# Keys of the last two token blocks as one product in seven half-size parts (Strassen), with both blocks' gates ahead of it

## The chip, the core and the metric

The kernel runs on one core of a Trainium2 chip. Times are device microseconds (us) of a whole execution; the number that counts is the median of several. In the profile PE is the matrix engine, PEld its weight loads, DVE the vector engine, ACT the scalar engine, POOL GpSimd, and SP the engine whose queue issues the DMAs.

## What is computed

Eight batches of a packed attention make `x` (4608 tokens of 512 channels), and a channel mix follows, whose products are the bulk of the work:

```python
x_prev = np.concatenate([zeros, x[:, :-1, :]], axis=1)
xk = mu_k * x + (1.0 - mu_k) * x_prev
xr = mu_r * x + (1.0 - mu_r) * x_prev
k = np.maximum(xk @ w_k, 0.0)              # 512 -> 1024: the keys
v = k * k @ w_v                            # 1024 -> 512: the values
r = 1.0 / (1.0 + np.exp(-(xr @ w_r)))      # 512 -> 512: the gates
return r * v
```

All in fp32. A factor that goes into a product is held as two fp32r parts, high and low, and a product is the sum of three matmuls: high by high, high by low, low by high.

## The kernel before

Tokens go in nine blocks of 512 (`TB`), numbered 0 to 8; channels in chunks of 128 (`P`). For a block, `gates(i)` makes 4 tiles of 4 chunks (48 matmuls with the three parts), `keys(i)` 8 tiles of 4 chunks (96), `values(i)` 4 tiles over 8 chunks (96): 240 matmuls of 128x512. `channel_mix` (L1267) runs gates, keys and values of block after block, and spawns the mixes of the next block (`mix`, `split`, L1091 and L1133) after the keys. A key tile `ph` is one bank of PSUM (a slot `m` of four); `squared` (L1169) then takes it by two ACT operations (L1173, L1176) and two on DVE (L1184, L1186) into `sq`, which `values` reads. `done` (L1247) multiplies a value tile by its gate on DVE (L1251) and issues the output DMA.

The attention of the batches is worked in between on the same engines and ends some 170 us before the kernel does. Its larger PSUM tiles, the two slots `pa`, are of two banks each: `banks(slot)` is `[P, 2, 512]`.

Nothing is scheduled at run time. `Flow` is a planner: each stage is a generator that yields an engine with an estimated duration, and the planner's estimates decide in which order the instructions are written, engine by engine. Each engine then runs its own instructions in that order and waits on semaphores which are put in from the tiles that an instruction reads and writes, in the order in which the instructions were written. A wait stands for all that follows on its engine.

Of the kernel before, what the change touches and what calls it, by code (L numbers as in the profile page):

```python
# [173 lines left out]
def attn_pack_channel_mix(ctx: ExitStack, tc: tile.TileContext, q, k, v, p, mu_k, mu_r, w_k, w_v, w_r, out):  # L174
    nc = tc.nc
    B, H, S, D = q.shape
    NP = p.shape[2]
    DM, DF = w_k.shape
    P = 128
# [5 lines left out]
    NC = DM // P  # L185
    NF = DF // P
    TB = 512
# [24 lines left out]
    def pe(us, after=None):  # L212
        return "tensor", us, after, None
# [877 lines left out]
    def mix(i, j, res, tag):  # L1091

        yield from flow.wait("mu")
        rank = flow.now.rank
        for c in range(NC):
            yield from flow.wait(*(
                e for b, *_ in pieces(i)
                for e in ([("xt", b, c, 0), ("xt", b, c, 1)] if b else [("kept", j // 2, c // 2)])
            ))
            slot = yield from flow.take("xk" if tag == "xk" else "sq")  # L1100

            space = "tmp"
# [49 lines left out]
    def keys(i):  # L1152
        for f in range(NF):
            slot = yield from flow.take("m")
            ph = ps.tile([P, 512], F32, name="ph", tag=f"m{slot}")[:, :TB]
            fs = slice(f * P, (f + 1) * P)
            for c in range(NC):
                yield from flow.wait(*made("xk", i, c), ("wk", c, f * P // WP * WP))
                yield pe(0.685)
                flow.now.t -= flow.LAG  # L1160
                _, xh, xl = xks[i, c]
                nc.tensor.matmul(ph, wk_h[:, c, fs], xh, start=(c == 0), stop=False)  # L1162
                nc.tensor.matmul(ph, wk_h[:, c, fs], xl, start=False, stop=False)  # L1163
# [3 lines left out]
            flow.spawn(squared(i, f, slot, ph), 0, flow.t + flow.LAG)  # L1167

    def squared(i, f, slot, ph):  # L1169
        sr = yield from flow.take("tmp")  # L1170
        r = tile_([P, WP], F32, "tmp", sr, "r")[:, :TB]
        yield act(TB)
        nc.scalar.activation(r, ph, AF.Relu)  # L1173
        flow.give("m", slot)
        yield act(TB)
        nc.scalar.activation(r, r, AF.Square)  # L1176
        sh = yield from flow.take("sq")
        hl = tile_([P, 2, TB], F32R, "sq", sh)
        if i < 1:
            yield act(TB, after=0.0)  # L1180
            nc.scalar.copy(hl[:, 0, :], r)  # L1181
        else:
            yield vec2(TB)
            nc.vector.tensor_copy(hl[:, 0, :], r)  # L1184
        yield vec(TB)
        nc.vector.tensor_tensor(hl[:, 1, :], r, hl[:, 0, :].bitcast(F32), op=ALU.subtract)  # L1186
        flow.give("tmp", sr)
        sqs[i, f] = sh, hl
        flow.set(("sq", i, f))
# [26 lines left out]
                flow.spawn(gated(i, x, slot, pr), 0, flow.t + flow.LAG)  # L1216

    def gated(i, t, slot, pr):
        sg = yield from flow.take("sig")
        sig = tile_([P, DM], F32, "sig", sg)  # L1220
        yield act(DM, table="sigmoid")
        nc.scalar.activation(sig, pr, AF.Sigmoid)  # L1222
        flow.give("m", slot)
        sigs[i, t] = sg, sig
        flow.set(("sig", i, t))

    def values(i):
        slots, pv = {}, {}
        for f in range(NF):
            yield from flow.wait(("sq", i, f), *(("wv", f, o) for o in range(0, DM, WP)))  # L1230
            sf, hl = sqs.pop((i, f))
            for t in range(NT):
# [12 lines left out]
            flow.give("sq", sf)  # L1245

    def done(i, t, slot, pv):  # L1247
        yield from flow.wait(("sig", i, t))
        sg, sig = sigs.pop((i, t))
        yield vec(DM)  # L1250
        nc.vector.tensor_tensor(sig, pv, sig, op=ALU.mult)  # L1251
        flow.give("m", slot)
        t0 = i * TB + t * P
        if t0 <= TB:

            runs_ = out[:S].rearrange("(r j) c -> j r c", j=RUN)
            for x, half in enumerate(HALVES):
# [7 lines left out]
        flow.give("sig", sg)  # L1265

    def channel_mix():  # L1267
        for i in range(NB):
# [4 lines left out]
            if i + 1 < NB:  # L1273
                mixes(i + 1)
            yield from values(i)

    def mixes(i):
        flow.spawn(mix(i, 2, xrs, "xr"), 1)
        flow.spawn(mix(i, 0, xks, "xk"), 1.1)

    def fronts():
        for b in range(B):
# [55 lines left out]
    flow.spawn(fronts(), 10)  # L1338
    weights()
    flow.spawn(shares(), 10.0)  # L1340
    flow.spawn(channel_mix(), 50)

    spare = ps.tile([P, 512], F32, name="spare", tag="m3")
# [31 lines left out]
```

## Time and profile before

| | us |
|---|---|
| runs, median of 3 (lowest to highest) | 590.94 (590.58 to 590.96) |
| span of the profiled execution, first to last instruction | 587.7 |
| median less that span | 3.2 |
| PE busy | 578.4 (98%) |
| DVE busy | 370.9 (63%) |
| ACT busy | 314.3 (53%) |

The time of the profiled execution itself is not among the runs; its span is, and the 3.2 us that the median has over it lie ahead of the first and behind the last instruction. PE's busy time counts a matmul from its start to its modelled end, and these overlap: the spacing of the starts is what an added or removed matmul costs. Idle time of the other engines costs nothing while PE has work.

### The profile page before, as it was taken

The numbers are of one execution on the slowest core, as the hardware profiler recorded it, in microseconds if no ns is written. First come the engines' busy times: TensorE is split into PE (matmuls) and PEld (weight loads), VectorE is DVE, ScalarE is ACT, GpSimd is POOL, SyncE is SP. The second block draws the span as 40 slices with busy tenths as digits, with TensorE's granted clock in tenths as the row PEclk, the third lists the DMA queues.
The fourth block names the chain that finished last, engine by engine and source line by source line (L and its number), as shares of the span: only waits on it lengthen the run. The fifth ranks groups of instructions, "written<-read, shape, count | busy, mean of one in ns | idle before, by whom it ended". The sixth has DMA issues, their size and how long they took to land.

```text
span 587.7 us, 10541 instructions
## 1 busy us (share of the span) xinstructions
PE 578.4 (98%) x4115; PEld 455.6 (78%) x4115; DVE 370.9 (63%) x702; ACT 314.3 (53%) x569; POOL 7.8 (1%) x33
## 2 busy tenths in 40 slices
PE   8999999999999999999999999999999999999997
PEld 7877777687788778777877777777788888888885
DVE  1999799956892888098828879559514713640321
ACT  5679974755744583368327654637535613721410
POOL 3000000000000000000000000000000000000000
PEclk9999999999999999999999999999999999999999
DMA  8987340863376365417621764820100010001001
GB/s 303 337 239 238 109 63 15 191 139 56 87 146 153 73 118 99 128 17 155 133 97 30 152 137 107 171 69 0 73 0 1 0 73 0 1 0 73 0 2 71
DMA packets 160593, 56.66 MB, mean 96 GB/s; under 512 B 136856, under 2 KB 150304, under 8 KB 160544
## 3 DMA queue, kind: packets, MB, share of 16 engines
q1 hardware_dynamic: 160224, 55.86, 37.8%
q8 instruction: 32, 0.52, 0.4%
q0 software_dynamic: 320, 0.14, 0.1%
q14 instruction: 17, 0.14, 0.1%
HBM read 43.00 MB, written 12.98 MB: 95 GB/s over the span
## 4 chain that ended last, share of the span: by engine, by line
PE 78%; DVE 13%; ACT 3%; DMA 3%; issue 2%; SPq 0%; DVEq 0%; ACTq 0%
PE ph L1162 10%; PE ph L1163 10%; PE ph L1164 10%; PE pvo L1240 9%; PE pvo L1242 9%; PE pvo L1241 9%; PE pr L1210 5%; PE pr L1212 5%; PE pr L1211 5%; PE pa L706 2%; DVE x L1117 2%; DVE m L303 2%; PE pa L898 1%; PE pa L672 1%; PE pa L841 1%
## 5 line engine op out<-in xcount | busy, mean ns | idle before, releaser
L1162 PE MATMUL ph<-xk,wk_h 128*128 128x512 f32 x288 | 115.6, 401 | 0.0
L1240 PE MATMUL pvo<-wv,sq 128*128 128x512 f32 x288 | 113.8, 395 | 0.0
L1163 PE MATMUL ph<-xk,wk_h 128*128 128x512 f32 x288 | 112.4, 390 | 0.0
L1164 PE MATMUL ph<-xk,wk_l 128*128 128x512 f32 x288 | 112.2, 390 | 0.0
L1241 PE MATMUL pvo<-wv,sq 128*128 128x512 f32 x288 | 112.2, 389 | 0.0
L1242 PE MATMUL pvo<-wv,sq 128*128 128x512 f32 x288 | 112.1, 389 | 0.0
L1184 DVE CAST sq<-r 128x512 fp32r<-128x512 f32 x64 | 27.0, 421 | 97.2 <-ACT r L1176 94.9
L1173 ACT ACTIVATE r<-ph 128x512 f32<-128x512 f32 x72 | 43.2, 600 | 77.8 <-PE ph L1164 75.7
L1162 PEld LDWEIGHTS ph<-xk,wk_h 128*128 128x128 f32 x288 | 54.0, 188 | 16.7 <-issue 5.9
L1240 PEld LDWEIGHTS pvo<-wv,sq 128*128 128x128 f32 x288 | 54.1, 188 | 16.0 <-issue 4.9
L1164 PEld LDWEIGHTS ph<-xk,wk_l 128*128 128x128 f32 x288 | 54.1, 188 | 11.4
L1242 PEld LDWEIGHTS pvo<-wv,sq 128*128 128x128 f32 x288 | 54.1, 188 | 11.3
L1241 PEld LDWEIGHTS pvo<-wv,sq 128*128 128x128 f32 x288 | 54.1, 188 | 10.7
L1163 PEld LDWEIGHTS ph<-xk,wk_h 128*128 128x128 f32 x288 | 54.2, 188 | 10.2 <-DVE xk L1056 0.2
L1210 PE MATMUL pr<-wr_h,xr 128*128 128x512 f32 x144 | 57.8, 402 | 0.7 <-ACT xr L1137 0.6
L1212 PE MATMUL pr<-wr_h,xr 128*128 128x512 f32 x144 | 56.3, 391 | 0.8 <-DVE xr L1139 0.8
L1211 PE MATMUL pr<-wr_l,xr 128*128 128x512 f32 x144 | 56.2, 390 | 0.0
L1117 DVE SCALAR_TENSOR_TENSOR x<-xt,mus,x 128x448 f32<-128x448 f32 (+6 forms) x112 | 52.4, 510 | 5.4 <-ACT x L1111 5.3
L1111 ACT ACTIVATE x<-xt,mus 128x448 f32<-128x448 f32 (+7 forms) x112 | 53.7, 527 | 2.4 <-DVE sq L1186 1.2
L1186 DVE TENSOR_TENSOR sq<-r,sq 128x512 fp32r<-128x512 f32 x72 | 49.1, 681 | 4.6 <-ACT sq L1181 3.3
L1222 ACT ACTIVATE sig<-pr 128x512 f32<-128x512 f32 x36 | 20.7, 598 | 54.2 <-PE pr L1212 42.1
L1176 ACT ACTIVATE r<-r 128x512 f32<-128x512 f32 x72 | 45.6, 633 | 1.7
(151 smaller groups left out, 679.5 us busy)
## 6 DMA issues: line engine op xcount, KB each, us to landing
out<-sig SPq DMA_DIRECT2D x31, 256.0 KB, 2.9
vt<-in_v SPq DMA_DIRECT2D x14, 512.0 KB, 4.9
raw<-in_k SPq DMA_DIRECT2D x96, 72.0 KB, 2.7
raw<-in_q SPq DMA_DIRECT2D x96, 72.0 KB, 2.8
st<-in_moe_w_k SPq DMA_DIRECT2D x8, 512.0 KB, 9.3
st<-in_moe_w_v SPq DMA_DIRECT2D x8, 512.0 KB, 5.7
far<-at SPq DMA_DIRECT2D x12, 288.0 KB, 2.6
aTd<-far SPq DMA_DIRECT2D x12, 256.0 KB, 2.9
```

The source lines that it names most:

```text
L1111: nc.scalar.mul(x32[:, o:o + n], xts[b, c][:, 1 + s:1 + s + n], mus[:, j, c:c + 1])
L1117: nc.vector.scalar_tensor_tensor(x32[:, o:o + n], xts[b, c][:, s:s + n], mus[:, j + 1, c:c + 1], x32[:, o:o + n], op0=ALU.mult, op1=ALU.add,)
L1162: nc.tensor.matmul(ph, wk_h[:, c, fs], xh, start=(c == 0), stop=False)
L1163: nc.tensor.matmul(ph, wk_h[:, c, fs], xl, start=False, stop=False)
L1164: nc.tensor.matmul(ph, wk_l[:, c, fs], xh, start=False, stop=(c == NC - 1))
L1186: nc.vector.tensor_tensor(hl[:, 1, :], r, hl[:, 0, :].bitcast(F32), op=ALU.subtract)
L1210: nc.tensor.matmul(pr, xh[:, ts_], wr_h[:, c, :], start=(c == 0), stop=False)
L1211: nc.tensor.matmul(pr, xh[:, ts_], wr_l[:, c, :], start=False, stop=False)
L1212: nc.tensor.matmul(pr, xl[:, ts_], wr_h[:, c, :], start=False, stop=(c == NC - 1))
L1240: nc.tensor.matmul(pv[t], sh, wvs[f][:, 0, :], start=(f == 0), stop=False)
L1241: nc.tensor.matmul(pv[t], sh, wvs[f][:, 1, :], start=False, stop=False)
L1242: nc.tensor.matmul(pv[t], sl, wvs[f][:, 0, :], start=False, stop=(f == NF - 1))
```

## The change

Take the two last blocks, 7 and 8, as one factor of 1024 tokens by 512 channels, in quarters: A11 and A12 are block 7's first and last 256 channels, and A21 and A22 block 8's. `w_k` is quartered alike (W11, W12, W21, W22, each 256 by 512). Instead of eight products of quarters there are seven, by Winograd's form of Strassen's scheme. S1 to S4 are sums of the A's, T1 to T4 sums of the W's; "pass" is one such product, 4 tiles of 2 chunks of 3 matmuls: 24 matmuls.

- `sums_of_w` makes T1 to T4 on DVE and ACT after the last batch's attention, in buffers that this has left free (T1 in the place of W12, which no pass reads).
- `quarters` replaces the mixes of both blocks: the gates' factors of both, then A in fp32, then the seven forms (A11, A12, S2, S3, S1, A22, S4) split in high and low on DVE. A form takes two `xt` slots, there are four: from the third on, a form can be written only when the pass two before it is done on PE.
- `channel_mix` runs, after block 6's values: gates of 7, gates of 8, the seven passes, values of 7, values of 8.
- `keys_of_pair` runs the passes. Those of Z go to four one-bank tiles (`ph`), those of X to the two two-bank tiles (`pa`), `X = [twin[j // 2][:, j % 2, :] for j in range(HF)]`. Some pass adds into a bank of an earlier one. What ACT keeps from Z (`kept`) DVE adds to X (`made_of`, three times four adds), and relu, square and split follow as before.
- The gates of block 8 stay in the `vt` buffers. No DMA is added or removed.

The core of the diff:

```diff
+        for i in PAIR:
+            yield from gates(i)
+        yield from keys_of_pair()
+        for i in PAIR:
+            yield from values(i)
...
+        yield from formed("A11", a)
+        yield from formed("A12", b)
+        forms["S2"] = yield from form_tiles()
+        for u in range(HC):
+            yield vec(TB)
+            nc.vector.tensor_tensor(c[:, u, :], a[:, u, :], c[:, u, :], op=ALU.subtract)
+            st_ = yield from flow.take("tmp")
+            s2 = tile_([P, TB], F32, "tmp", st_, "s2")
+            yield vec(TB)
+            nc.vector.tensor_tensor(s2, d[:, u, :], c[:, u, :], op=ALU.subtract)
+            yield from parted_form("S2", s2, u)
+            yield vec(TB)
+            nc.vector.tensor_tensor(a[:, u, :], a[:, u, :], s2, op=ALU.add)
+            yield vec(TB)
+            nc.vector.tensor_tensor(b[:, u, :], b[:, u, :], s2, op=ALU.subtract)
+            flow.give("tmp", st_)
+        for name, x, slot in (("S3", c, sc), ("S1", a, sa), ("A22", d, sd), ("S4", b, sb_)):
+            yield from formed(name, x)
+            flow.give("xk", slot)
...
+    def parted_form(name, x, u):
+        (_, h), (_, l) = forms[name]
+        yield vec2(TB)
+        nc.vector.tensor_copy(h[:, u, :], x)
+        yield vec(TB)
+        nc.vector.tensor_tensor(l[:, u, :], x, h[:, u, :].bitcast(F32), op=ALU.subtract)
+        flow.set((name, u))
...
+        def made_of(bank, j, i, h, n):
+            yield from flow.wait(("home", i, h))
+            to = rest(i, h, j)
+            if n is None:
+                yield act(TB)
+                nc.scalar.activation(to, bank[j], AF.Relu)
+                flow.give("m", ms[j])
+            else:
+                yield from flow.wait(("kept", n, j))
+                yield vec(TB)
+                nc.vector.tensor_tensor(to, bank[j], to, op=ALU.add)
+                flow.set(("read", i, h, j))
...
+        passes = (
+            ("A11", own(0, 0), Z, True, None, lambda j: kept("P1", j, first, 0)),
+            ("A12", own(HC, 0), X, True, None, lambda j: made_of(X, j, first, 0, "P1")),
+            ("S2", summed(T2), Z, False, "P1", lambda j: kept("U2", j, first, 1)),
+            ("S3", summed(T3), Z, False, "U2", lambda j: kept("U3", j, second, 1)),
+            ("S1", summed(T1), X, True, (first, 0), lambda j: made_of(X, j, second, 1, "U3")),
+            ("A22", summed(T4), Z, False, "U3", lambda j: made_of(Z, j, second, 0, None)),
+            ("S4", own(HC, WP), X, False, (second, 1), lambda j: made_of(X, j, first, 1, "U2")),
+        )
...
+                for u in range(HC):
+                    yield from flow.wait((name, u))
+                    (_, xh), (_, xl) = forms[name]
+                    yield pe(0.685)
+                    flow.now.t -= flow.LAG
+                    wh, wl = ws[u][0][:, js], ws[u][1][:, js]
+                    nc.tensor.matmul(bank[j], wh, xh[:, u, :], start=(opens and u == 0), stop=False, skip_group_check=(not opens))
+                    nc.tensor.matmul(bank[j], wh, xl[:, u, :], start=False, stop=False, skip_group_check=(not opens))
+                    nc.tensor.matmul(bank[j], wl, xh[:, u, :], start=False, stop=(u == HC - 1), skip_group_check=(not opens))
+                flow.spawn(evict(j), 0, flow.t + flow.LAG)
```

PE before, keys of block 8, from the last chunk of one key tile to the next tile (`ph`); `xk` is the factor's chunk, `_h` and `_l` the weights' parts. Names carry buffer numbers, and a bracket the engines that a row waits for:

```order
L1162 MATMUL ph_5729<-xk_5581,wk_h_127 128x512
L1163 MATMUL ph_5729<-xk_5581,wk_h_127 128x512
L1164 MATMUL ph_5729<-xk_5581,wk_l_128 128x512
L1162 MATMUL ph_5744<-xk_5531,wk_h_127 128x512 [waits Activation_49]
L1163 MATMUL ph_5744<-xk_5531,wk_h_127 128x512
L1164 MATMUL ph_5744<-xk_5531,wk_l_128 128x512
```

PE now, second pass (A12 into X), second tile and the start of the third: `pa_5506` is the tile with banks X[0] and X[1], `pa_5507` that with X[2] and X[3], `form_5474` and `form_5475` are A12's high and low part:

```order
L1551 MATMUL pa_5506<-form_5474,wk_h_127 128x512
L1552 MATMUL pa_5506<-form_5475,wk_h_127 128x512
L1553 MATMUL pa_5506<-form_5474,wk_l_128 128x512
L1551 MATMUL pa_5506<-form_5474,wk_h_127 128x512 [waits DVE_49]
...
L1551 MATMUL pa_5507<-form_5474,wk_h_127 128x512 [waits PE_49]
```

Before, a key tile waits once, at its first matmul, for the bank to be free. Now there is a wait for DVE in the middle of the tile X[1], at its fourth matmul.

DVE before, keys of block 8, the first tiles' squares (`r` is what ACT wrote):

```order
L1251 TENSOR_TENSOR sig_5360<-pvo_5528,sig_5360 128x512 [waits DMAHW5_49,PE_49]
L1184 CAST sq_5753<-r_5743 128x512 [waits Activation_49]
L1186 TENSOR_TENSOR sq_5753<-r_5743,sq_5753 128x512 [waits DVE_49]
L1184 CAST sq_5772<-r_5762 128x512 [waits Activation_49]
L1186 TENSOR_TENSOR sq_5772<-r_5762,sq_5772 128x512 [waits DVE_49]
```

DVE now, from the start of S2's first half to the last pass that it stands ahead of, S3 (`xq` are A's quarters in fp32, `form_5543` and `form_5544` S2's parts, `q` what ACT kept, to which X is added):

```order
L1397 TENSOR_TENSOR s2_5546<-xq_5418,xq_5417 128x512 [waits DVE_49]
L1419 CAST form_5543<-s2_5546 128x512 [waits DVE_49,PE_49]
L1484 TENSOR_TENSOR q_5508<-pa_5506,q_5508 128x512 [waits PE_49,Activation_49]
L1421 TENSOR_TENSOR form_5544<-s2_5546,form_5543 128x512 [waits DVE_49]
L1484 TENSOR_TENSOR q_5508<-pa_5506,q_5508 128x512 [waits PE_49,Activation_49]
L1400 TENSOR_TENSOR xq_5347<-xq_5347,s2_5546 128x512
L1402 TENSOR_TENSOR xq_5348<-xq_5348,s2_5546 128x512
L1484 TENSOR_TENSOR q_5509<-pa_5507,q_5509 128x512 [waits PE_49,Activation_49]
L1393 TENSOR_TENSOR xq_5417<-xq_5347,xq_5417 128x512
L1484 TENSOR_TENSOR q_5509<-pa_5507,q_5509 128x512 [waits Activation_49]
L1397 TENSOR_TENSOR s2_5585<-xq_5418,xq_5417 128x512 [waits DVE_49]
L1419 CAST form_5543<-s2_5585 128x512 [waits DVE_49]
```

Counted by the semaphores' values, the first of these four adds (L1484) waits for X[1]'s third matmul, and X[1]'s fourth waits for this add. The third add (X[2]) waits for the last matmul of the pass, and behind it stand three 128x512 operations and the cast of S2's second half.

PE now, at the third pass (S2 into Z), which reads these forms (`T2` are the parts of T2):

```order
L1553 MATMUL pa_5507<-form_5474,wk_l_128 128x512
L1551 MATMUL ph_5502<-form_5543,T2_4911 128x512 [waits Activation_49]
L1552 MATMUL ph_5502<-form_5544,T2_4911 128x512 [waits DVE_49]
L1553 MATMUL ph_5502<-form_5543,T2_4912 128x512
L1551 MATMUL ph_5502<-form_5543,T2_4918 128x512 [waits DVE_49]
L1552 MATMUL ph_5502<-form_5544,T2_4918 128x512 [waits DVE_49]
```

The fourth matmul of the pass waits for the cast of S2's second half and the fifth for its subtraction (L1421). The other passes into X, the fifth and the seventh, have the wait in the middle of X[1] and in the middle of X[3]; the second has it in X[1] alone. PE's order up to block 6's gates is that of before, and it has 24 matmuls fewer behind them.

## Rows read from the trace of the kernel before

**Rows 1.** Page, the span in 40 slices: PE's busy tenths and its granted clock.

```profile
PE   8999999999999999999999999999999999999997
PEclk9999999999999999999999999999999999999999
```

**Rows 2.** Waits of PE, whole span: who waited for whom, us in total, times, longest.

```profile
PE pr L1212 <- DVE xr L1139: 0.8, 2, 0.4
PE pr L1210 <- ACT xr L1137: 0.6, 1, 0.6
```

**Rows 3.** Last three blocks: length, busy (count) of PE, PEld, DVE, ACT, POOL, PEclk, DMA.

```profile
419.50:474.97 55.47, 55.47 (x253) 45.79 (x245) 23.87 (x46) 26.70 (x47) 0.00 (x0) 1.00 0.06 22
475.00:529.40 54.40, 54.40 (x242) 45.06 (x241) 22.01 (x37) 21.82 (x36) 0.00 (x0) 1.00 0.05 20
529.40:583.90 54.50, 54.47 (x241) 44.78 (x239) 11.79 (x21) 12.23 (x20) 0.00 (x0) 1.00 0.06 21
```

**Rows 4.** Timeline of PE in the keys of block 6: start, duration, engine, line.

```profile
440.23 0.39 PE L1162 MATMUL ph<-xk,wk_h 128*128 128x512 f32 x1
440.45 0.39 PE L1163 MATMUL ph<-xk,wk_h 128*128 128x512 f32 x1
440.68 0.39 PE L1164 MATMUL ph<-xk,wk_l 128*128 128x512 f32 x1
440.91 0.39 PE L1162 MATMUL ph<-xk,wk_h 128*128 128x512 f32 x1
```

**Rows 5.** Chain of work that ended last, its last step.

```profile
583.90 0.69 DVE sig L1251
```

**Rows 6.** Timeline, from a matmul to the engine that reads its bank, two places.

```profile
442.04 0.39 PE L1164 MATMUL ph<-xk,wk_l 128*128 128x512 f32 x1
442.47 0.60 ACT L1173 ACTIVATE r<-ph 128x512 f32<-128x512 f32 x1 [1.46 <-PE ph L1164]
442.49 0.39 PE L1163 MATMUL ph<-xk,wk_h 128*128 128x512 f32 x1
...
581.44 0.39 PE L1242 MATMUL pvo<-wv,sq 128*128 128x512 f32 x1
581.87 2.73 DVE L1251 TENSOR_TENSOR sig<-pvo,sig 128x512 f32<-128x512 f32 x4 [17.27 <-PE pvo L1242]
```

**Rows 7.** Timeline around PE's last wait for DVE, at 113 us.

```profile
112.34 0.68 DVE L1139 TENSOR_TENSOR xr<-x,xr 128x512 fp32r<-128x512 f32 x1
113.08 0.19 PEld L1212 LDWEIGHTS pr<-wr_h,xr 128*128 128x128 f32 x1 [0.85 <-DVE xr L1139]
113.08 0.50 PE L1212 MATMUL pr<-wr_h,xr 128*128 128x512 f32 x1 [0.41 <-DVE xr L1139]
113.42 0.39 PE L1210 MATMUL pr<-wr_h,xr 128*128 128x512 f32 x1
```

**Rows 8.** Groups of DVE, 425 to 584 us: busy, mean ns, idle before, releaser.

```profile
L1186 DVE TENSOR_TENSOR sq<-r,sq 128x512 fp32r<-128x512 f32 x24 | 16.6, 692 | 0.8
L1184 DVE CAST sq<-r 128x512 fp32r<-128x512 f32 x24 | 10.2, 427 | 74.0 <-ACT r L1176 72.4 <-PE pvo L1242 1.6
L1251 DVE TENSOR_TENSOR sig<-pvo,sig 128x512 f32<-128x512 f32 x12 | 8.2, 692 | 28.7 <-PE pvo L1242 28.7
L1117 DVE SCALAR_TENSOR_TENSOR x<-xt,mus,x 128x512 f32<-128x512 f32 x8 | 5.9, 748 | 0.9 <-ACT x L1111 0.9
```

**Rows 9.** Timeline of DVE: a cast and the subtraction that waits for it.

```profile
441.04 0.43 DVE L1184 CAST sq<-r 128x512 fp32r<-128x512 f32 x1 [1.57 <-ACT r L1176]
441.50 0.69 DVE L1186 TENSOR_TENSOR sq<-r,sq 128x512 fp32r<-128x512 f32 x1
```

**Rows 10.** Groups of ACT, 425 to 584 us, the same columns.

```profile
L1173 ACT ACTIVATE r<-ph 128x512 f32<-128x512 f32 x24 | 14.4, 598 | 35.8 <-PE ph L1164 35.8
L1111 ACT ACTIVATE x<-xt,mus 128x512 f32<-128x512 f32 x8 | 5.7, 718 | 0.0
```

**Rows 11.** Window around PE's last waits, columns as in rows 3.

```profile
110.00:114.00 4.00, 2.86 (x10) 1.64 (x10) 4.00 (x8) 3.69 (x7) 0.10 (x1) 1.00 0.84 190
```

More of the change, by code (lines that the diff above doesn't have):

```diff
@@ L1167, in keys @@
             flow.spawn(squared(i, f, slot, ph), 0, flow.t + flow.LAG)
+        flow.set(("keys", i))
     def squared(i, f, slot, ph):
@@ L1218, in gated @@
     def gated(i, t, slot, pr):
-        sg = yield from flow.take("sig")
-        sig = tile_([P, DM], F32, "sig", sg)
+        if i == NB - 1:
+            if not t % 2:
+                vt = yield from flow.take("vt")
+                late_sig[t // 2] = vt, tile_([P, 2, DM], F32, "vt", vt, "sigs")
+                flow.set(("late sig", t // 2))
+            yield from flow.wait(("late sig", t // 2))
+            sg, sig = None, late_sig[t // 2][1][:, t % 2, :]
+        else:
+            sg = yield from flow.take("sig")
+            sig = tile_([P, DM], F32, "sig", sg)
         yield act(DM, table="sigmoid")
@@ L1231, in values @@
             sf, hl = sqs.pop((i, f))
+            tag = "sq" if i not in PAIR else "xk" if f < NF // 2 else "xt"
             for t in range(NT):
@@ L1244, in values @@
                     flow.spawn(done(i, t, slots[t], pv[t]), 0, flow.t + flow.LAG)
-            flow.give("sq", sf)
+            flow.give(tag, sf)
     def done(i, t, slot, pv):
@@ L1264, in done @@
             yield from load(out[t0:t0 + P, :], sig, 0.63, 0.75)
-        flow.give("sig", sg)
+        if sg is not None:
+            flow.give("sig", sg)
     def channel_mix():
-        for i in range(NB):
+        for i in range(NB - 2):
             if i == 0:
@@ L1272, in channel_mix @@
             yield from keys(i)
-            if i + 1 < NB:
-                mixes(i + 1)
+            mixes(i + 1)
+            yield from values(i)
[3 more added lines that the diff above has]
+        for i in PAIR:
             yield from values(i)
     def mixes(i):
-        flow.spawn(mix(i, 2, xrs, "xr"), 1)
-        flow.spawn(mix(i, 0, xks, "xk"), 1.1)
+        if i not in PAIR:
+            flow.spawn(mix(i, 2, xrs, "xr"), 1)
+            flow.spawn(mix(i, 0, xks, "xk"), 1.1)
+            return
@@ new lines, in mixes, with retired @@
+        flow.spawn(quarters(), 1)
+    PAIR = NB - 2, NB - 1
+    HF, HC = NF // 2, NC // 2
+    late_sig = {}
+    LEAD = dict(
+        raw=(0, 0, 0), kq=(0, 64, 0, 64), a=(0, 64), a2=(0,), e=(64, 0), aT=(64,), vt=(64, 64), xt=(64, 56, 48, 8),
+    )
+    def retired():
+        yield from flow.wait(("px", B - 1, 0), ("px", B - 1, 1))
+        for tag in ("kq", "raw", "a", "a2", "e", "aT"):
+            for _ in range(BUFS[tag]):
+                slot = yield from flow.take(tag)
+                flow.give("small", (tag, slot))
+        for u in range(HC):
+            flow.spawn(sums_of_w(u), 40 + u)
@@ new lines, in attn_pack_channel_mix, with sums_of_w, whole, add @@
+    small = {}
+    T2, T3, T4, T1 = "T2", "T3", "T4", "T1"
+    def sums_of_w(u):
+        vt = yield from flow.take("vt")
+        ws = tile_([P, 2, WP], F32, "vt", vt, "ws")
+        x, y = ws[:, 0, :], ws[:, 1, :]
+        hl = {}
+        for name in (T3, T2, T4):
+            for part in range(2):
+                tag, slot = yield from flow.take("small")
+                o = LEAD[tag][slot]
+                hl[name, part] = tile_([P, S], F32R, tag, slot, name)[:, o:o + WP]
+            small[name, u] = hl[name, 0], hl[name, 1]
+        def whole(to, c, o):
+            yield vec(WP)
+            nc.vector.tensor_tensor(
+                to, wk_h[:, c, o:o + WP].bitcast(F32), wk_l[:, c, o:o + WP].bitcast(F32), op=ALU.add,
+            )
+        def add(to, a, b, op):
+            yield vec(WP)
+            nc.vector.tensor_tensor(to, a, b, op=op)
+        def parted(to, raw):
+            yield act(WP)
+            nc.scalar.copy(to[0], raw)
+            yield vec(WP)
+            nc.vector.tensor_tensor(to[1], raw, to[0].bitcast(F32), op=ALU.subtract)
+        yield from whole(x, HC + u, WP)
+        yield from whole(y, u, WP)
+        s3 = yield from flow.take("tmp")
+        t3 = tile_([P, WP], F32, "tmp", s3, "t3")
+        yield from add(t3, x, y, ALU.subtract)
+        yield from whole(x, u, 0)
+        s2 = yield from flow.take("tmp")
+        t2 = tile_([P, WP], F32, "tmp", s2, "t2")
+        yield from add(t2, t3, x, ALU.add)
+        yield from parted(small[T3, u], t3)
+        flow.give("tmp", s3)
+        yield from add(y, y, x, ALU.subtract)
+        yield from whole(x, HC + u, 0)
+        yield from add(x, x, t2, ALU.subtract)
+        yield from parted(small[T2, u], t2)
+        flow.give("tmp", s2)
+        yield from parted(small[T4, u], x)
+        for name in (T2, T3, T4):
+            flow.set((name, u))
+        yield from flow.wait(("keys", NB - 3))
+        small[T1, u] = wk_h[:, u, WP:], wk_l[:, u, WP:]
+        yield from parted(small[T1, u], y)
+        flow.set((T1, u))
+        flow.give("vt", vt)
@@ new lines, in attn_pack_channel_mix, with quarters @@
+    forms = {}
+    def quarters():
+        yield from mix(PAIR[0], 2, xrs, "xr")
+        yield from mix(PAIR[1], 2, xrs, "xr")
+        flow.now.rank = 1.1
+        A, slots = {}, {}
+        for i in PAIR:
+            for h in range(2):
+                slots[i, h] = yield from flow.take("xk")
+                A[i, h] = tile_([P, HC, TB], F32, "xk", slots[i, h], "xq")
+            yield from mixed_whole(i, 0, [A[i, c // HC][:, c % HC, :] for c in range(NC)])
+        (a, b), (c, d) = ((A[i, 0], A[i, 1]) for i in PAIR)
+        (sa, sb_), (sc, sd) = ((slots[i, 0], slots[i, 1]) for i in PAIR)
+        yield from formed("A11", a)
[17 more added lines that the diff above has]
+            flow.give("xk", slot)
@@ new lines, in form_tiles @@
+    def form_tiles():
+        got = []
+        for part in range(2):
+            slot = yield from flow.take("xt")
+            o = LEAD["xt"][slot]
+            got.append((slot, tile_([P, 2 * (S + 1)], F32R, "xt", slot, "form")[:, o:o + HC * TB].rearrange("p (u t) -> p u t", u=HC)))
+        return got
+    def parted_form(name, x, u):
[4 more added lines that the diff above has]
+        nc.vector.tensor_tensor(l[:, u, :], x, h[:, u, :].bitcast(F32), op=ALU.subtract)
+        flow.set((name, u))
@@ new lines, in formed, with mixed_whole @@
+    def formed(name, x):
+        forms[name] = yield from form_tiles()
+        for u in range(HC):
+            yield from parted_form(name, x[:, u, :], u)
+    def mixed_whole(i, j, tiles):
+        for c in range(NC):
+            yield from flow.wait(*(e for b, *_ in pieces(i) for e in [("xt", b, c, 0), ("xt", b, c, 1)]))
+            for b, s, n, o in pieces(i):
+                yield act(n)
+                nc.scalar.mul(tiles[c][:, o:o + n], xts[b, c][:, 1 + s:1 + s + n], mus[:, j, c:c + 1])
+            for b, s, n, o in pieces(i):
+                yield vec(n)
+                nc.vector.scalar_tensor_tensor(
+                    tiles[c][:, o:o + n], xts[b, c][:, s:s + n], mus[:, j + 1, c:c + 1], tiles[c][:, o:o + n],
+                    op0=ALU.mult, op1=ALU.add,
+                )
+                if s + n == S:
+                    left = xt2[b, c // 2]
+                    left[2] -= 1
+                    if not left[2]:
+                        flow.give("xt", left[0])
@@ new lines, in keys_of_pair, with home, rest, kept @@
+    def keys_of_pair():
+        ms, pas = [], []
+        for j in range(HF):
+            ms.append((yield from flow.take("m")))
+        Z = [ps.tile([P, TB], F32, name="ph", tag=f"m{slot}") for slot in ms]
+        pas = yield from two_slots()
+        twin = [banks(slot) for slot in pas]
+        X = [twin[j // 2][:, j % 2, :] for j in range(HF)]
+        Q = {}
+        def home(i, h):
+            for g in range(HF // 2):
+                slot = yield from flow.take("sq")
+                Q[i, h, g] = slot, tile_([P, 2, TB], F32, "sq", slot, "q")
+            flow.set(("home", i, h))
+        def rest(i, h, j):
+            return Q[i, h, j // 2][1][:, j % 2, :]
+        def kept(n, j, i, h):
+            yield from flow.wait(("home", i, h))
+            yield act(TB)
+            nc.scalar.copy(rest(i, h, j), Z[j])
+            flow.set(("kept", n, j))
+        def made_of(bank, j, i, h, n):
+            yield from flow.wait(("home", i, h))
+            to = rest(i, h, j)
+            if n is None:
+                yield act(TB)
+                nc.scalar.activation(to, bank[j], AF.Relu)
+                flow.give("m", ms[j])
+            else:
+                yield from flow.wait(("kept", n, j))
+                yield vec(TB)
+                nc.vector.tensor_tensor(to, bank[j], to, op=ALU.add)
+                flow.set(("read", i, h, j))
+                if (i, h) == (PAIR[0], 1) and j % 2:
+                    flow.give("pa", pas[j // 2])
+                yield act(TB)
+                nc.scalar.activation(to, to, AF.Relu)
+            yield act(TB)
+            nc.scalar.activation(to, to, AF.Square)
+            flow.set(("r", i, HF * h + j))
+        def squares():
+            for i in PAIR:
+                for f in range(NF):
+                    yield from flow.wait(("r", i, f))
+                    tag = "xk" if f < HF else "xt"
+                    slot = yield from flow.take(tag)
+                    o = LEAD[tag][slot] if tag == "xt" else 0
+                    size = 2 * (S + 1) if tag == "xt" else 2 * TB
+                    hl = tile_([P, size], F32R, tag, slot, "hl")[:, o:o + 2 * TB].rearrange("p (u t) -> p u t", u=2)
+                    flow.spawn(parted_square(i, f, slot, hl), 0)
+        def parted_square(i, f, slot, hl):
+            raw = rest(i, f // HF, f % HF)
+            yield vec2(TB)
+            nc.vector.tensor_copy(hl[:, 0, :], raw)
+            yield vec(TB)
+            nc.vector.tensor_tensor(hl[:, 1, :], raw, hl[:, 0, :].bitcast(F32), op=ALU.subtract)
+            sqs[i, f] = slot, hl
+            flow.set(("sq", i, f))
+        flow.spawn(squares(), 0.5)
+        first, second = PAIR
+        for h in range(2):
+            flow.spawn(home(first, h), 0)
+            flow.spawn(home(second, 1 - h), 0)
+        def own(c, o):
+            return [(wk_h[:, c + u, o:o + WP], wk_l[:, c + u, o:o + WP]) for u in range(HC)], ()
+        def summed(name):
+            return None, [(name, u) for u in range(HC)]
+        passes = (
[6 more added lines that the diff above has]
+            ("S4", own(HC, WP), X, False, (second, 1), lambda j: made_of(X, j, first, 1, "U2")),
+        )
+        for n, (name, (ws, events), bank, opens, before, evict) in enumerate(passes):
+            yield from flow.wait(*events)
+            if ws is None:
+                ws = [small[events[u]] for u in range(HC)]
+            for j in range(HF):
+                if isinstance(before, str):
+                    yield from flow.wait(("kept", before, j))
+                elif before:
+                    yield from flow.wait(("read", *before, j))
+                js = slice(j * P, (j + 1) * P)
+                for u in range(HC):
+                    yield from flow.wait((name, u))
[7 more added lines that the diff above has]
+                flow.spawn(evict(j), 0, flow.t + flow.LAG)
+            for slot, _ in forms[name]:
+                flow.give("xt", slot)
@@ L1340, in attn_pack_channel_mix @@
     flow.spawn(shares(), 10.0)
+    flow.pool("small", 0)
+    flow.spawn(retired(), 35)
     flow.spawn(channel_mix(), 50)
```

## The prediction, made before the changed kernel ran

> **What bounds the kernel now.** The slices come first: PE reads 9 in all of them but the ends, and its granted clock stays at the full level, 2.4 GHz [rows 1]. Then PE's waits: those of the channel mix are 0.8 and 0.6 us in all, the last of them at 113 us [rows 2, 7]. So the stage of the change has to be read by itself. In the windows of the last three blocks PE is busy for all of the time, DVE for 23.87 of 55.47, 22.01 of 54.40 and 11.79 of 54.50 us [rows 3]. The timeline shows what a matmul costs there: three of them take 440.91 - 440.23 = 0.68 us from start to start, 0.227 each [rows 4]; the 0.39 us of a row is its length, two thirds of which another covers. The chain ends with DVE's last multiplication, right behind PE [rows 5]. A matmul that goes is then worth 0.227 us, and DVE and ACT cost nothing, unless PE has to wait for them. The question is whether it now does.
>
> **What is removed.** The keys of the two blocks are 192 matmuls; seven passes of 24 are 168. The 24 that go stand on the path: 8 x 0.68 = **5.44 us less**.
>
> **What costs nothing, and under what cover.** (a) The sums of the weights are 24 operations of 0.69 us on DVE (L1186) [rows 8], 16.6 us, and 8 casts on ACT. All but the two for T1 come while block 6's gates and keys run, where DVE has 31.6 us to spare [rows 3]. Behind them in DVE's queue stand block 6's squares, which PE wants only after its 96 key matmuls, 21.8 us on. (b) The factors of both gates are mixed ahead of A; those of block 8 are wanted 48 matmuls, 10.9 us, after those of block 7. (c) A11's form must be there when both gates are done, 96 matmuls or 21.8 us after block 6's values. The last mixing operation on ACT stands behind the sigmoid of block 8's first gate tile, which ends with matmul 60 at 13.6 us. From there 0.2 us to ACT, 0.60 and 0.72 on ACT [rows 10], 0.75 on DVE (L1117) [rows 8] and two halves of 0.43 + 0.69 with their gaps [rows 8, 9] give 18.2 us: 3.6 us of slack. Were it gone, each microsecond would show on PE. (d) The later forms S3, S1, A22 and S4 have a pass of 24 x 0.227 = 5.4 us each, and want 2.3 us of DVE; what ACT keeps from Z (0.60 us) has most of a pass until it is added into. (e) The end is as before: four tiles, four multiplications, four output DMAs.
>
> **The waits inside a tile.** In X the add of one bank and the matmuls into its neighbour are chained by the program's waits, as the order shows: the add waits for the neighbour's third matmul, and its fourth for the add. Nothing can run on PE meanwhile, as all that follows stands behind the fourth. This round trip is not in the trace of before as one piece, so I put it together. From the start of the third matmul to the start of a DVE operation that reads PSUM: 581.87 - 581.44 = 0.43 us [rows 6]. The add has the form of L1251 (PSUM and SBUF in, 128x512): 0.69 [rows 8]. From the end of a DVE operation to PE's weight load: 113.08 - (112.34 + 0.68) = 0.06, and from there to the next matmul's start 113.42 - 113.08 = 0.34 [rows 7]. Together 1.52 us between two starts that lie two matmuls, 0.45, apart when nothing waits: 1.07 us a time. There are five of them (second pass X[1], fifth and seventh X[1] and X[3]): **5.35 us more**. From below: if the waiting matmul's weights are loaded already, 0.34 becomes 0.23 and a wait 0.96. From above: DVE may still be in the cast that stands ahead of the add, 0.43 more [rows 8]; I take that for at most two of the five, since in the second and fifth passes the casts ahead of it are done before the ninth matmul is.
>
> Here the Trainium skill speaks against the charge. In before, PE goes on at 442.49 in one key tile while ACT reads the tile before it at 442.47 [rows 6], each in a bank of its own, with no wait. "PSUM — Partial Sum Buffer" (section on the summary of rules for kernel authors) says the same: a bank may be read while a matmul runs in a different bank, and semaphores should guard by bank. X[0] and X[1] are different banks, so by that rule the term is nothing instead of 5.35, and the sum 588.9 (below). I charge it all the same, because the program has the wait whether the chip needs it or not.
>
> **S2's second half.** The third pass wants it at its fourth matmul, and its making stands in DVE's queue behind the add of X[2], which waits for the last matmul of the second pass. With that matmul's start at 0: the add starts at 0.43; then add, subtraction, add, subtraction at 0.69, a gap of 0.03 [rows 9] and the cast of 0.43 [rows 8] end at 3.66; PE's fourth matmul follows 0.06 later, and the fifth would start at 4.06 (both gaps [rows 7]) instead of 5 x 0.227 = 1.13: 2.92 us. The fifth waits for the subtraction, 0.03 + 0.69 later, which leaves 0.49 more: **3.41 us**. Below, without the weight load (twice 0.11): 3.2. Above, with one more 0.69 us operation between: 4.1. For the fourth pass S3 is ready: two subtractions, a cast and a subtraction, 2.5 us, against 20 matmuls, 4.5 us.
>
> **Sum.** 5.35 + 3.41 - 5.44 = +3.3 us. The profiled execution's span goes from 587.7 to 591.0, and with the 3.24 us that the median has over the span, to **594.3 us**, 0.56% slower. By its own bounds: 5 x 0.96 + 3.2 - 5.44 = +2.6, or 5.35 + 2 x 0.43 + 4.1 - 5.44 = +4.9, so 593.5 to 595.8.
>
> **The rivals.** *The waits between neighbouring banks cost nothing* (faster). The mechanism is that PE's fourth matmul finds the add done: the add would have to be out before the third matmul of the neighbour has ended. For it speaks that PE and ACT work on neighbouring banks at once in before [rows 6]; against it the order, where the add itself waits for that third matmul. Then only S2's 3.41 is left: 590.94 - 5.44 + 3.41 = 588.9. It decides where a wait is under (5.44 - 3.41) / 5 = 0.41 us.
>
> *Neither waits* (faster): DVE keeps up as in the keys of before, where it idles before each cast (74.0 us over 24 [rows 8]). All of the removed work is then gained: 585.5. Against it: DVE's queue holds four adds and S2 between the same two matmuls.
>
> *Only S2 comes in time* (no change): the five waits stand, DVE's three SBUF operations fall into PE's pauses. 590.94 - 5.44 + 5.35 = 590.9. Against it: the add of X[2] waits for the pass's end, and what S2 still needs lies behind.
>
> *The clock falls* (slower still): PE stands for 2.9 us in the third pass. Before, the clock was granted in full through the 1.14 us of pauses at 110 to 114 us (4.00 less 2.86 [rows 11]); no row shows a longer one at work. At 1.2 GHz a matmul would cost 0.227 more; over the 20 that are left of the third pass that is 4.5 us: 598.8. The Trainium skill, "TensorE: Matmul & The Clock Gate" (section on HAM oscillation), tells of kernels in which pauses between bursts of matmuls take the clock to half; by that the rival is real, but no run here shows it.
>
> *The change does not do what it says* hardly comes up: PE's order has 24 matmuls fewer, and all of it up to block 6's gates as it was.
>
> **How the numbers follow.** The forecast 0.75, since each of its two terms is a wait that stands in the order, with durations from rows; neighbouring waits free 0.10 (588.9), neither 0.04 (585.5), only S2 in time 0.06 (590.9), clock 0.05 (598.8). A measurement of this kernel tells some 0.2%, 1.2 us, from no change. Faster is 0.10 + 0.04 = 0.14, same 0.06, slower 0.75 + 0.05 = 0.80. Leaving out the two fast cases and the clock is 0.19, so the range runs from the unchanged case to a little over the forecast's own upper bound: 590.8 to 596.0. The forecast's own range is 593.5 to 595.8.
>
> **What would show it.** PE's waits should name DVE on the matmul's line five times at about 1.1 us for the adds, and twice, 2.9 and 0.5, for S2's cast and subtraction, and nothing else after 120 us. The last window from block 6's values to the end should have PE idle for some 8 to 9 us. If PE is not idle there and the span is shorter by about 5, the waits are free and my reading of the order is wrong. If there are waits at the first, fourth or sixth pass, slack (c) or (d) was wrong. A granted clock under full after the third pass would be the last rival.

## The result, and the profile after

| | before | after |
|---|---|---|
| median us (lowest to highest, 5 runs each) | 590.58 (590.32 to 590.96) | 595.34 (594.82 to 596.15) |
| span of the profiled execution | 587.7 | 593.6 |

The changed kernel is slower: ratio 1.0084, 95% interval 1.0072 to 1.0096, or 4.8 us. The forecast was 594.3.

The page's slices of the kernel after, as [rows 1]:

```profile
PE   7999999999999999999999999999999999788997
DVE  1999799857792997198738877659865564766421
PEclk9999999999999999999999999999999999899999
```

Against before, PE has gaps in three slices near the end, and in one of them the granted clock is below its full level. The waits of PE in the kernel after (who waited for whom, us in total, times, longest):

```profile
PE pa L1551 <- DVE q L1484: 4.1, 5, 0.9
PE ph L1551 <- DVE form L1419: 2.4, 1, 2.4
PE ph L1552 <- DVE form L1421: 0.2, 1, 0.2
PE pr L1211 <- DVE sig L1261: 0.3, 1, 0.3
```

The first three are new, and they are the five adds and S2's cast and subtraction that the prediction names. The view counts idle time by the modelled ends of matmuls, so it shows less than a wait costs; the cost is read from start to start. (The last is early in the kernel, beside those of [rows 2].) Windows of the kernel after, from the attention's end to the second pass, over the passes and the values' start, and to the last matmul:

```profile
420.00:503.70 83.70, 83.70 (x384) 68.97 (x383) 51.93 (x91) 43.09 (x75) 0.00 (x0) 1.00 0.07 26
503.70:550.00 46.30, 39.51 (x160) 30.38 (x159) 30.59 (x55) 24.18 (x41) 0.00 (x0) 0.96 0.00 1
550.00:589.80 39.80, 39.80 (x176) 32.63 (x174) 12.70 (x23) 0.00 (x0) 0.00 (x0) 1.00 0.08 31
```

All of the idle time is in the middle one, 46.30 - 39.51 = 6.79 us (the prediction's 8 to 9 were counted by starts): the sums of the weights, both blocks' gates and the values run as full as the blocks did in [rows 3].

**One wait inside a tile of X.** The timeline at the second pass (start, duration, engine, line, and in brackets the idle time before with what ended it):

```profile
504.83 0.39 PE L1553 MATMUL pa<-form,wk_l 128*128 128x512 f32 x1
505.32 0.69 DVE L1484 TENSOR_TENSOR q<-pa,q 128x512 f32<-128x512 f32 x1 [1.68 <-PE pa L1553]
506.07 0.19 PEld L1551 LDWEIGHTS pa<-form,wk_h 128*128 128x128 f32 x1 [1.28 <-DVE q L1484]
506.07 0.50 PE L1551 MATMUL pa<-form,wk_h 128*128 128x512 f32 x1 [0.85 <-DVE q L1484]
506.41 0.40 PE L1552 MATMUL pa<-form,wk_h 128*128 128x512 f32 x1
```

From 504.83 to 506.41 is 1.58 us where two matmuls take 0.45: 1.12 us. Read in the same way, the two in the fifth pass are 1.12 each, and the two in the seventh 1.05: **5.46 us** for the five, against 5.35 in the sum. The weight load starts only when the add has ended, as the row of PEld shows; it is not ahead of the wait.

**S2's second half.** The timeline from the last matmul ahead of it:

```profile
510.06 0.39 PE L1553 MATMUL ph<-form,T 128*128 128x512 f32 x1
...
512.88 0.49 PE L1551 MATMUL ph<-form,T 128*128 128x512 f32 x1 [2.43 <-DVE form L1419]
513.61 0.50 PE L1552 MATMUL ph<-form,T 128*128 128x512 f32 x1 [0.23 <-DVE form L1421]
513.94 0.40 PE L1553 MATMUL ph<-form,T 128*128 128x512 f32 x1
```

2.82 - 0.23 = 2.59, then 0.50 and 0.10 over: **3.19 us** (the sum had 3.41). DVE in the same stretch:

```profile
503.22 0.43 DVE L1419 CAST form<-s 128x512 fp32r<-128x512 f32 x1 [6.02 <-PE ph L1553]
...
509.87 0.69 DVE L1484 TENSOR_TENSOR q<-pa,q 128x512 f32<-128x512 f32 x1 [0.84 <-PE pa L1553]
510.48 0.68 DVE L1393 TENSOR_TENSOR xq<-xq 128x512 f32<-128x512 f32 x1
511.08 0.68 DVE L1484 TENSOR_TENSOR q<-pa,q 128x512 f32<-128x512 f32 x1
511.68 0.68 DVE L1397 TENSOR_TENSOR s<-xq 128x512 f32<-128x512 f32 x1
512.39 0.43 DVE L1419 CAST form<-s 128x512 fp32r<-128x512 f32 x1
```

The add of X[2], the difference, the add of X[3], the sum and the cast, in the order that was written. The first row shows what this costs: DVE had stood for 6.02 us during the first pass, at the cast of S2's first half, with the sums of the second half behind it that need no room.

**The clock.** After S2's pause PE's matmuls of the third pass are 0.43 apart for a while:

```profile
514.18 0.39 PE L1551 MATMUL ph<-form,T 128*128 128x512 f32 x1
514.41 0.54 PE L1552 MATMUL ph<-form,T 128*128 128x512 f32 x1
514.74 0.63 PE L1553 MATMUL ph<-form,T 128*128 128x512 f32 x1
515.17 0.63 PE L1551 MATMUL ph<-form,T 128*128 128x512 f32 x1
515.59 0.63 PE L1552 MATMUL ph<-form,T 128*128 128x512 f32 x1
...
517.73 0.48 PE L1551 MATMUL ph<-form,T 128*128 128x512 f32 x1
518.05 0.39 PE L1552 MATMUL ph<-form,T 128*128 128x512 f32 x1
```

In windows (the clock is the third column from the right) it is the granted clock, 0.95 and then 0.71 where [rows 3] have 1.00, a mixture of the full 2.4 GHz and of 1.2:

```profile
510.00:515.00 5.00, 2.33 (x8) 1.37 (x8) 4.93 (x9) 3.02 (x5) 0.00 (x0) 0.95 0.00 0
515.00:520.00 5.00, 5.00 (x17) 3.98 (x17) 2.93 (x6) 1.17 (x2) 0.00 (x0) 0.71 0.00 0
```

Nine spacings are longer, from 514.41 to 518.05: 3.64 us where nine take 2.04, **1.60 us** more. In the five runs the mean clock was 0.997, 0.997, 0.996, 0.999 and 0.997, and the one at 0.999 is the fastest.

**The account.** From the last matmul of the attention (419.07 before, 420.00 after, with the same order of PE's instructions up to there) to the last of the kernel the time grew by 5.0 us. The terms give 5.46 + 3.19 + 1.60 - 5.44 = 4.81. The 0.2 that are left belong to no one wait: the other spacings, some 670, are 0.2269 us on average where before's are 0.2267.

```profile
420.00 0.67 PE pa L898 x16
```

The 0.9 us ahead of that say nothing of the change: over the profiles of this study, one of each kernel, the attention's last matmul lies anywhere from 419.1 to 421.2.

### The profile page after: what moved, and what is told of

The parts are those of the page before. It is cut to its first block, busy times and chain, and to the rows that moved or that the text cites. A ratio compares the mean times of both kernels' runs of the same rounds, so it can differ in the third digit from the quotient of the medians.

```text
span 593.6 us, 10565 instructions
## 1 busy us (share of the span) xinstructions
PE 576.8 (97%) x4091; PEld 451.6 (76%) x4091; DVE 407.7 (69%) x766; ACT 321.1 (54%) x581; POOL 7.8 (1%) x33
## 4 chain that ended last, share of the span: by engine, by line
PE 73%; DVE 16%; DMA 4%; ACT 3%; issue 2%; SPq 1%; DVEq 0%; ACTq 0%
PE pvo L1250 8%; PE pvo L1251 8%; PE pvo L1252 8%; PE ph L1162 8%; PE ph L1163 7%; PE ph L1164 7%; PE pr L1211 5%; PE pr L1213 5%; PE pr L1212 5%; DVE x L1117 2%; PE pa L706 2%; DMA st<-in_moe_w_r 1%; PE ph L1552 1%; PE ph L1553 1%; PE ph L1551 1%
## 5 line engine op out<-in xcount | busy, mean ns | idle before, releaser
L1162 PE MATMUL ph<-xk,wk_h 128*128 128x512 f32 x224 | 90.7, 405 | 0.0
L1250 PE MATMUL pvo<-wv,sq 128*128 128x512 f32 x224 | 89.0, 397 | 0.0
L1163 PE MATMUL ph<-xk,wk_h 128*128 128x512 f32 x224 | 87.5, 391 | 0.0
L1164 PE MATMUL ph<-xk,wk_l 128*128 128x512 f32 x224 | 87.3, 390 | 0.0
L1251 PE MATMUL pvo<-wv,sq 128*128 128x512 f32 x224 | 87.3, 390 | 0.0
L1252 PE MATMUL pvo<-wv,sq 128*128 128x512 f32 x224 | 87.2, 389 | 0.0
L1162 PEld LDWEIGHTS ph<-xk,wk_h 128*128 128x128 f32 x224 | 42.0, 188 | 14.3 <-issue 5.9
L1250 PEld LDWEIGHTS pvo<-wv,sq 128*128 128x128 f32 x224 | 42.1, 188 | 13.6 <-issue 4.9
L1117 DVE SCALAR_TENSOR_TENSOR x<-xt,mus,x 128x128 f32<-128x128 f32 (+6 forms) x100 | 46.5, 504 | 4.7 <-ACT x L1111 4.5
L1252 PEld LDWEIGHTS pvo<-wv,sq 128*128 128x128 f32 x224 | 42.0, 188 | 9.0
L1164 PEld LDWEIGHTS ph<-xk,wk_l 128*128 128x128 f32 x224 | 42.0, 188 | 9.0
L1251 PEld LDWEIGHTS pvo<-wv,sq 128*128 128x128 f32 x224 | 42.1, 188 | 8.1
L1111 ACT ACTIVATE x<-xt,mus 128x128 f32<-128x128 f32 (+6 forms) x100 | 47.6, 522 | 1.2 <-DVE sq L1187 1.2
L1163 PEld LDWEIGHTS ph<-xk,wk_h 128*128 128x128 f32 x224 | 42.1, 188 | 7.6 <-DVE xk L1056 0.2
L1187 DVE TENSOR_TENSOR sq<-r,sq 128x512 fp32r<-128x512 f32 x56 | 38.0, 679 | 4.1 <-ACT sq L1182 3.3
L1072 ACT COPY xt<-pa 128x576 f32<-128x576 f32 x28 | 30.6, 1173 | 10.8 <-PE pa L898 10.7
```

Source lines behind the costliest of these rows:

```text
L1117: nc.vector.scalar_tensor_tensor(x32[:, o:o + n], xts[b, c][:, s:s + n], mus[:, j + 1, c:c + 1], x32[:, o:o + n], op0=ALU.mult, op1=ALU.add,)
```

## The experiments

Two theories. **The waits**: the 24 matmuls are gained in full, and the program's own waits, with the low clock behind one of them, take more back. **The rival**: the pauses are only where a slower whole comes to light (DVE is behind, or the new order costs something), so that removing one moves it. The kernel of before ran again beside each group of experiments: medians are compared with 590.33 us (13 runs) for the first four, and with 590.77 (17 runs) for the last three. The changed kernel itself was timed only once, beside 590.58, so a distance to its 595.34 can be off by 0.2 to 0.3 us.

### The adds behind their neighbours

```diff
-                flow.spawn(evict(j), 0, flow.t + flow.LAG)
+                held.append(evict(j))
+                if bank is Z or j % 2:
+                    for part in held:
+                        flow.spawn(part, 0, flow.t + flow.LAG)
+                    held = []
```

> The add of an even bank of X is written only when its neighbour's six matmuls stand, so that no matmul waits for it; S2 as in the changed kernel. Theory (the five waits inside X's tiles cost 5.5 us as the trace of the changed kernel shows them): these rows are gone, time falls from 595.3 to about 590 us; S2's wait stays, a little shorter (2.3 to 2.6 us, since DVE is less behind), and whether the clock falls after it shows if that needs S2's pause alone. Rival (the pauses only make room for DVE, which is behind): the five waits go but PE waits elsewhere, at S2 and the passes after it, time stays at 594 to 595.5 us.

Measured: 589.08 us, ratio 0.997 (0.9959 to 0.998): faster than before, 6.3 us under the changed kernel. PE's waits in the last 165 us:

```profile
PE ph L1552 <- DVE form L1419: 1.8, 1, 1.8
PE ph L1553 <- DVE form L1421: 0.2, 1, 0.2
```

The five are gone and no wait came in their place. Of S2's the rows are:

```profile
510.08 0.39 PE L1554 MATMUL ph<-form,T 128*128 128x512 f32 x1
512.30 0.50 PE L1552 MATMUL ph<-form,T 128*128 128x512 f32 x1 [1.83 <-DVE form L1419]
```

That is a pause of 2.22 us from start to start, and with the next two spacings S2 costs 2.59 us here. The seven runs: 587.69, 587.87 and 589.07 with the clock at 1.000, and 589.08 to 589.58 with 0.997. In the profiled one, 589.07, PE's clock was full all through; there the attention ended at 421.18, later than in any other profile. So with S2's pause alone, without the five, the clock is below full in four executions of seven. None of these four was profiled: that the fall comes behind S2's pause, as in the kernel after, is inferred, and a later experiment fills this pause to see.

### S2 summed early

```diff
-        forms["S2"] = yield from form_tiles()
+        sums = []
         for u in range(HC):
...
-            yield from parted_form("S2", s2, u)
+            sums.append((st_, s2))
+        forms["S2"] = yield from form_tiles()
+        for u in range(HC):
+            yield from parted_form("S2", sums[u][1], u)
+        for u in range(HC):
+            st_, s2 = sums[u]
```

> Both halves of S2 are summed before the A11 pass is done, so that only cast and subtraction are left for the time after it; the adds of X stay as in the changed kernel, and the order now has six waits inside X's tiles, one more. Theory: S2's 3.2 us and the 1.8 us of the low clock go, one wait of 1.1 us comes, 595.3 - 5.0 + 1.1 = 591.5 us, and the clock is granted in full throughout. Rival (the low clock comes from all the short pauses together): the clock still falls, 593 us.

Measured: 592.31 us, ratio 1.0033 (1.0021 to 1.0045); the clock at 0.999 or 1.000 in all runs.

```profile
PE pa L1556 <- DVE q L1489: 5.0, 6, 0.9
```

S2's waits are gone, a sixth wait is there, and the six are 6.62 us by starts; the short pauses alone took the clock down in none of the six runs. The median lies 0.8 us over the expectation. Of this 0.2 is the low clock, which was put at 1.8 there and took 1.60. The rest stays open: in the profiled execution no spacing of the passes beyond the six waits is long, and 1.1 us of that profile's distance to before's come ahead of the attention's end.

### Both

> Both edits together: no matmul waits for an add or for S2. Theory (the waits and the low clock behind them are all that stands between the changed kernel and its 24 matmuls): PE without a wait in the last 110 us, 590.6 - 5.4 = 585.2 us. Rival (the sums, the forms and the other order cost something more, by contention or ahead of the passes): 587 us or more with PE's spacing over 0.227 us or waits at the gates.

Measured: **585.48 us**, ratio 0.9913 (0.99 to 0.9926), 4.9 us under before. PE waits for nothing from 420 us on, and the window of its passes, against the middle one of the kernel after:

```profile
502.00:540.00 38.00, 38.00 (x170) 31.45 (x169) 28.49 (x52) 23.32 (x42) 0.00 (x0) 1.00 0.00 1
```

This decides between the two theories: no matmul waits for sums, forms, copies or the order of the stages, and the 24 matmuls are worth what they were put at, within the interval (4.4 to 5.9 us against 5.44). It is the fastest version here; late adds alone beat the kernel before too, by less.

### S2's pause filled

Eleven matmuls with zero weights (`none`, made ahead by one DVE operation), in the pause:

```diff
+                    if (name, j, u) == ("S2", 0, 0):
+                        for _ in range(11):
+                            nc.tensor.matmul(bank[j], none, xh[:, u, :], start=False, stop=False, skip_group_check=True)
```

> The changed kernel with eleven matmuls of zero weights, which add nothing, put into S2's pause ahead of the fourth matmul of the third pass; its wait still ends when DVE is done. Theory (1.8 us of the changed kernel's time are the low clock after S2's pause, no wait): the clock stays full, 595.3 - 1.8 = 593.5 us. Rival (the slow matmuls after the pause have another cause, such as the forms being written at the time): the ten slow matmuls are still there, 595.3 us.

Measured: 593.68 us, ratio 1.0054 (1.0041 to 1.0067), 1.7 us under the changed kernel (1.4 when each is counted from the median of before that ran beside it), with the clock at 0.999 or 1.000 in all runs. The timeline where the kernel after stood:

```profile
510.16 2.65 PE L1560 MATMUL ph<-form,none 128*128 128x512 f32 x11
512.75 0.49 PE L1555 MATMUL ph<-form,T 128*128 128x512 f32 x1
513.48 0.50 PE L1556 MATMUL ph<-form,T 128*128 128x512 f32 x1 [0.23 <-DVE form L1421]
513.82 0.40 PE L1557 MATMUL ph<-form,T 128*128 128x512 f32 x1
514.06 0.40 PE L1555 MATMUL ph<-form,T 128*128 128x512 f32 x1
```

S2's cast comes at the same time, and the matmuls behind it keep 0.23 to 0.24 us. DVE and ACT do the same work as in the kernel after; only PE's standing is gone. So the slow matmuls are the clock's, and the clock's fall is the pause's.

### The gates ahead alone

```diff
-        yield from keys_of_pair()
         for i in PAIR:
+            yield from keys(i)
             yield from values(i)
...
-        flow.spawn(quarters(), 1)
+        flow.spawn(plain_mixes(), 1)
```

`plain_mixes` mixes the gates' factors of both blocks, then the keys'. The keys of 7 and 8 are made by `keys(i)` as in the kernel before, 192 matmuls, which is what the expectation calls eight half-size products.

> Only the other order of the stages: the gates of blocks 7 and 8 first, with both their factors mixed ahead, then keys and values of 7 and of 8 as eight half-size products, no sums of weights, no forms. Theory (moving the gates costs nothing on PE): 590.4 us, no wait in the last 110 us. Rival (part of the loss is the gates' order): 591.5 us or more, with waits at the gates of block 8 or the keys of 8.

Measured: 590.80 us, ratio 1.0002 (0.9994 to 1.0011), and PE without a wait from 420 us on. This part of the change costs nothing that the interval (0.4 us down to 0.6 up) can tell, as was forecast.

### Late adds and a filled pause

> As the kernel whose adds come behind the neighbour's matmuls, with eight matmuls of zero weights in S2's pause. Theory (that kernel's runs fall in two groups, 587.7 to 587.9 with the clock at 1.000 and 589.1 to 589.6 with it at 0.997, because the clock falls after a pause of some 2.2 us in some executions and not in others): all runs have the clock at 0.999 or above, the median is 587.8 us. Rival (the two groups have another cause): the groups stay.

Measured: 588.14 us (587.44 to 588.75), ratio 0.996 (0.9947 to 0.9973), the clock at 0.999 or above in all five. The group with the low clock is gone, so S2's pause brought it, as far as five runs tell. The median is 0.9 us under the unfilled one, or 1.4 when each is counted from the median of before that ran beside it; the groups of the first experiment lie some 1.4 apart (587.7 and 587.9 against 589.1 to 589.6). The runs still spread over 1.3 us with the clock full, so the time of a single run does not tell on which side it was.

### X and Z change places

```diff
-        Z = [ps.tile([P, TB], F32, name="ph", tag=f"m{slot}") for slot in ms]
+        X = [ps.tile([P, TB], F32, name="ph", tag=f"m{slot}") for slot in ms]
...
-        X = [twin[j // 2][:, j % 2, :] for j in range(HF)]
+        Z = [twin[j // 2][:, j % 2, :] for j in range(HF)]
```

> X in the four one-bank tiles and Z in the two tiles of two banks; all else as in the changed kernel. Theory (a wait follows the two-bank tile, whatever reads it): the five waits for DVE's adds are gone, and in their place the order has eight for ACT, which takes Z's banks in four passes, each 0.43 + 0.60 + 0.06 + 0.34 - 0.45 = 0.98 us; S2's wait is some 2.7 us. 590.4 - 5.4 + 7.8 + 2.7 = 595.5 us, and up to 1.8 more where the clock falls. Rival (DVE's adds are late in any case): waits for DVE at X stay, waits for ACT are short, 595 us with five DVE waits.

Measured: 597.00 us, ratio 1.0107 (1.0085 to 1.0128). PE's waits:

```profile
PE pa L1552 <- ACT q L1471: 4.1, 6, 0.7
PE pa L1552 <- DVE form L1419: 1.5, 1, 1.5
PE pa L1552 <- ACT q L1479: 1.4, 2, 0.7
PE pa L1553 <- DVE form L1421: 0.2, 1, 0.2
```

The five waits for adds are gone, and eight for ACT stand in their place, 0.94 to 0.96 us each by starts; S2 costs 2.3 us where 2.7 was expected. The wait goes with the tile of two banks and not with the engine that reads it, nor with DVE being late. The six runs are two groups again: 595.03 to 595.64 with the clock at 1.000, as the sum had it, and 598.36 to 599.06 at 0.994, and the median of 597.00 stands between them. Here the low clock takes some 3 us, twice as much as in the kernel after, and its mean is twice as far below full (0.006 against 0.003).

## Why the prediction was right

- **Removed: 5.44 us.** Right: with the waits away the kernel is 4.9 us faster (interval 4.4 to 5.9), and the spacing of matmuls did not change. (The prediction says that another matmul covers two thirds of a row of 0.39 us. The next one covers 0.39 - 0.227 = 0.16, some two fifths; no term rests on it.)
- **What costs nothing.** Right for each: the gates ahead alone change nothing; the window up to the second pass is full; and A11's form was done at 493.73 when the first pass began at 497.58, a slack of 3.9 us where 3.6 was worked out. The rows are DVE's last subtraction of A11 and PE's first matmul:

```profile
493.04 0.69 DVE L1421 TENSOR_TENSOR form<-xq,form 128x512 fp32r<-128x512 f32 x1
...
497.58 0.39 PE L1551 MATMUL ph<-form,wk_h 128*128 128x512 f32 x1
```

- **The waits inside a tile, 5.35 us.** Right in number, place and size (5.46), and shown twice, by taking them away and by moving them to the other tiles. The rival that the bank rule speaks for did not come about: the program has the wait, and it is obeyed. Whether PE could write one bank of such a tile while DVE reads the other, no run here shows. The Trainium skill's "PSUM — Partial Sum Buffer" (summary of rules) says to guard by bank; here the guard was by tile, and that is what cost the 5.46 us.
- **S2, 3.41 us.** Right in place, 0.2 too high (3.19 measured): four DVE operations in a row, of which each was put at 0.69, start 0.60 to 0.71 apart. It does not come by itself in time, as the rival had it.
- **The clock.** This is the step that failed. It was given one chance in twenty as a case apart, at 4.5 us. It came on top of the forecast case, in at least four runs of five, at 1.60 us in the profile: the rest of the third pass is 20 matmuls, each put at 0.227 more, but the clock was full again after nine spacings, of which the slowest were 0.20 longer. With 0.1 more for the adds and 0.2 less for S2 this is the 1.4 us by which the measured difference (4.8) is over the forecast one (3.3), and the filled pause gives 1.4 to 1.7 back. The sum had no term for it. That the median still lies within the forecast's own range, 593.5 to 595.8, is luck: its upper end stood for casts ahead of the adds and for one more operation ahead of S2, and neither came. The row that it was weighed by, pauses of 1.14 us in four microseconds with the clock full [rows 11], says nothing of one pause of 2.8.
- **The time around the span.** The 3.24 us put there are 2.2 by the run that was profiled after (595.77 against a span of 593.6), and by the runs of before in the experiments (590.27 against 588.1). So some 2.2 us of the 3.2 lie outside the span, and the rest is that the profiled execution of before was about 1 us shorter than the median. As the sum added a difference to the median, nothing came of it.

## What to carry to other kernels

Where two halves of one buffer are filled and emptied in turn, look at the program's order for a wait in the middle of the second half: give each half its own tile, or write the reading of the first behind the filling of the second. And make what needs no room ahead of the wait for room: here the sums of S2 stood 6 us behind a cast that waited for a buffer. With both, a saving of 24 matmuls that had turned into a loss of 4.8 us became a gain of 4.9.

## What the runs showed of the hardware

A pause of PE can cost more than its length, and not in each execution. In the profile of the changed kernel the clock granted after a pause of 2.82 us from start to start was 0.71 of full in a window of 5 us, between the levels of 2.4 and 1.2 GHz, and at least four of its five runs had the mean clock at 0.996 or 0.997. With a pause of 2.22 (first experiment) it was four runs of seven, at 0.997. Six pauses of 1.17 to 1.24 us, whose starts lie 3.8 us or more apart (S2 summed early), took the clock down in none of six runs. In the last experiment, with S2's pause at 1.91 us among eight of 1.07, three of six runs had it at 0.994. Which of two equal executions the clock falls in is not in the program. Where it falls in the last experiment, and whether once or twice, stays open: only a run with the full clock was profiled there.
